# Another schedule for decoding weights and for fill matmuls in the attention stage of a fused attention and gated MLP kernel

## The chip, the core and the metric

The kernel runs on one core of a Trainium2 chip. The metric is device time in microseconds (us) of one execution; the kernel before took 1249.73 us (median of three runs, 1249.0 to 1255.0). The core's engines are called PE (matrix multiply; PEld its weight loads), DVE (vector), ACT (activation), POOL (GpSimd) and SP, whose queue issues every transfer here.

## What is computed

Random-feature attention, then a gated MLP on its output, all in float32; the MLP's weights come as float64.

```python
proj = q_or_k @ w_phi                        # 8 batches x 8 heads, 576 rows, 64 -> 128 features
proj = proj - max(abs(proj), axis=-1)
phi  = concat([exp(proj), exp(-proj)])       # 256 features
kv, z = phi(k).T @ v, sum(phi(k))            # per head
x  = (phi(q) @ kv) / (phi(q) @ z + 1e-6)     # then as 4608 tokens x 512
xn = x / sqrt(mean(x*x) + 1e-6) * rms_g
out = (silu(xn @ w_gate) * (xn @ w_val)) @ w_out      # 512 -> 1536 -> 512
```

## The kernel before, in words

There are three stages. The attention stage handles two heads of a batch at a time, a *pair*; 32 pairs (`PR`) go through a pipeline of four steps in a loop of 35 *rounds*. In round i, `front(i)` transposes q and k of pair i (L298), projects them (L311 to L313: three matmuls, since float32 is split in a high and a low part), and takes the row maximum (L315) and the difference (L318) on DVE. `mid(i-1)` makes the exponentials on ACT (L341, L345, L381, L382), the low parts of the q features on POOL (L386, L388), and phi(k).T v on PE (L349, L354), whose result is split by L60 and L61. `back(i-2)` multiplies with phi(q) (L421), copies the result out (L424, L429), and sends the denominators through memory for a reciprocal (L431, L438, L440, L441, L443). `last(i-3)` scales on DVE (L458, L459) and stores 576 tokens of x.

Two kinds of work of the second stage ride along in these rounds:

- *Decoding.* The float64 weights are turned into float32 by integer operations. A *piece* is one 128 x 384 block: a load of 384 KB (L37), two passes on ACT (L48, L49), three on DVE (L50 to L52), two on POOL (L54) and a last sum on DVE (L55). There are 32 pieces. The first eight are kept in SBUF as operands of the fills: for them `fill_w` adds a scaling by g (L234) and a split (L60 on ACT, L61 on DVE, tiles fg and fv). The other 24 are stored to memory (L240) and are read back later, for the first time by L157 and L161 (`raw_gv`, tile wc).
- *Fills.* A *unit* is twelve matmuls of 256 columns (L490), a product of 256 finished tokens with 128 decoded columns of w_gate or w_val, copied out by ACT (L493) and stored (L494). Six units belong to a block of 256 tokens, which is loaded (L507) and split (L60, L61, tile xo) once. 54 units are done in the attention stage and the other 54 after it.

How many of each go in a round is set by three statements of the loop: `dq` adds up a quota of pieces per round, `FIRST` is the first round with fills, and `quota` spreads 40 units evenly over the rounds from `FIRST` to 31 and 14 over the last three. `_merge` sorts the round's pieces of work by a position between 0 and 1 and issues them in that order. On top of that the framework's scheduler reorders instructions by its own estimates of durations; so it also puts two DVE operations on tile wc, which belong to the next stage, into the attention rounds. Every engine runs its own instructions strictly in the order that results.

The second stage (L566, L1041 to L1076) does the rest of the fills and the gated product by a Strassen-Winograd scheme with 7 products; the third (L1257) is the product with w_out.

Of the kernel before, what the change touches and what calls it, by code (L numbers as in the profile page):

```python
# [63 lines left out]
def _merge(streams):  # L64


    todo = []
    for n, st in enumerate(streams):
        for i, piece in enumerate(st):
            at = (i + 0.5) / len(st)  # L70
            if isinstance(piece, tuple):
                at, piece = piece
            todo.append((at, n, i, piece))
    for _, _, _, piece in sorted(todo, key=lambda t: t[:3]):
        piece()


def _spread(pieces, a, b):
    return [(a + (b - a) * (n + 0.5) / len(pieces), p) for n, p in enumerate(pieces)]
# [3 lines left out]
def kernel(ctx: ExitStack, tc: tile.TileContext, q, k, v, w_phi,  # L83
# [14 lines left out]
    J1 = 3  # L98
# [54 lines left out]
    def raw_gv(j):  # L153

        raws[j] = w = wst.tile([128, 5, 2, 128], F32, name="wc")
        cs = slice((J1 + j) * 128, (J1 + j + 1) * 128)
        nc.sync.dma_start(out=w[:, 0:2].rearrange("p o c f -> p (o c) f"),  # L157
                          in_=wgs[:, cs].rearrange("(c p) f -> p c f", p=128))
        vv = wvs[:, cs].rearrange("(k c p) f -> k p c f", p=128, c=2)
        for k in range(2):  # L160
            nc.sync.dma_start(out=w[:, 3 - k], in_=vv[k])  # L161
# [90 lines left out]
    def decode_pieces(jobs, dec):  # L252
        raws = {}

        def piece(i):
            if i == 0:
                raws[0] = _fetch(nc, dec, *jobs[0][:2])
            raw = raws.pop(i)
            if i + 1 < len(jobs):
                raws[i + 1] = _fetch(nc, dec, *jobs[i + 1][:2])  # L260
            with late():
                jobs[i][2](_decode(nc, dec, raw, jobs[i][1], nc.gpsimd if i >= 2 * NC + 24 else nc.vector))
        return [lambda i=i: piece(i) for i in range(len(jobs))]
# [3 lines left out]
    def load(pr):  # L267
        b, hp = divmod(pr, NP)
        h0 = 2 * hp
        kt = ld.tile([128, 2, T0, D], F32, name="kt")  # L270
        qt = ld.tile([128, 2, T0, D], F32, name="qt")
        for dst, src in ((kt, k), (qt, q)):
            nc.sync.dma_start(out=dst.rearrange("p h t d -> p h (t d)"),
                              in_=src[b, h0:h0 + 2, 0:SM, :].rearrange("h (p t) d -> p h (t d)", t=T0))
        rb = ld.tile([128, 2, D], F32, name="rb")
        vm, vr = vms[pr % 3], vrs[pr % 3]
        for i, src in enumerate((k, q)):
            nc.sync.dma_start(out=rb[:, i], in_=src[b, h0:h0 + 2, SM:S, :])
        for hh in range(2):
            nc.sync.dma_start(out=vm[:, hh, :, 0:D], in_=v[b, h0 + hh, 0:SM, :].rearrange("(p t) d -> p t d", t=T0))  # L280
            nc.sync.dma_start(out=vr[hh * 64:(hh + 1) * 64, hh, 0:D], in_=v[b, h0 + hh, SM:S, :])
        st[pr] = dict(kt=kt, qt=qt, rb=rb, hp=hp, b=b, vm=vm, vr=vr, kv=kvs[pr % 2])
# [167 lines left out]
    def last(pr):  # L450
        d = st.pop(pr)
        nd, rc, b, hp = d["nd"], d["rc"], d["b"], d["hp"]

        def fin():
            xt = nd[0]
            eng = nc.gpsimd if pr == PR - 2 else nc.vector
            with late():
                eng.tensor_tensor(xt[0:64], nd[0][0:64], rc[:, 0], ALU.mult)  # L458
                eng.tensor_tensor(xt[64:128], nd[1][0:64], rc[:, 1], ALU.mult)  # L459
            r0, c0 = hp * 128, b * S  # L460
            if b % 2 == 0:
                nc.sync.dma_start(out=xs[r0:r0 + 128, c0:c0 + S], in_=xt)
            else:
                nc.sync.dma_start(out=xs[r0:r0 + 128, c0:c0 + SR], in_=xt[:, SM:S])
                nc.sync.dma_start(out=xs[r0:r0 + 128, c0 + SR:c0 + S], in_=xt[:, 0:SM])
            if hp == NP - 1:
                while blocks and blocks[0] * TF + TF <= (b + 1) * S:
                    fills.append(blocks.pop(0))

        return [(0.65, fin)]  # L470
# [25 lines left out]

    early = decode_jobs()
    decs = decode_pieces(early, dec)
    RES, FIRST, TAIL = 9 * J1 * 2, 9, 14
    units, here = [], []  # L500
    dq = quota = 0.0

    def load_x():
        while fills and len(here) < 2:
            bk = fills.pop(0)
            x = fxp.tile([128, NC, TF], F32, name="x")
            nc.sync.dma_start(out=x, in_=xsv[:, :, bk * TF:(bk + 1) * TF])  # L507
            here.append((bk, x))
# [3 lines left out]
    def landed(lo_eng=nc.vector):  # L512
        if here:
            units.extend(fill(*here.pop(0), lo_eng, [fp, fp]))
# [4 lines left out]
    for i in range(PR + 3):  # L519
        streams = []  # L520
        if i < PR:
            streams.append(_spread(front(i), -0.2, 0.7))
        if 0 <= i - 1 < PR:
            streams.append(_spread(mid(i - 1), -0.2, 1.1))
        if 0 <= i - 2 < PR:
            streams.append(back(i - 2))
        if 0 <= i - 3 < PR:
            streams.append(last(i - 3))
        dq += 0.8 if i < 10 else 1.1
        dl, decs = decs[:int(dq)], decs[int(dq):]  # L530
        dq -= int(dq)
        streams.append(dl)
        if i < PR:
            _merge(streams)
        if len(units) <= 6:
            landed(nc.vector if i < PR else nc.gpsimd)
        if i >= FIRST:
            quota += (N // TF * J1 * 2 - RES - TAIL) / (PR - FIRST) if i < PR else TAIL / 3
            nf = min(int(quota + 1e-6), len(units))
            quota -= nf  # L540
            now, units[:] = units[:nf], units[nf:]
            _merge([now] if i < PR else streams + [_spread(now, 0.0, 0.75)])
        load_x()
        if i + 2 < PR:
            load(i + 2)
        if i in (20, 22):
            raw_gv((i - 20) // 2)
# [780 lines left out]
```

## Time and profile before

| what | value |
|---|---|
| median of the runs | 1249.73 us |
| the profiled execution's own time | 1250.33 us |
| its span, first to last instruction | 1248.6 us |
| PE busy | 1216.2 us (97%) |
| DVE, ACT, POOL busy | 1034.0, 803.3, 830.8 us |
| mean granted PE clock | 0.991 |
| end of the attention stage, about | 507 us |

The profile gives busy times of each engine, the chain of work that ended last, groups of instructions with what ended the idle time before them, and tables of stretches in which the number behind an x counts instructions. Ends of matmuls are modelled, so a busy PE may still be waiting for short times; the count of matmuls in a stretch is the better measure there.

### The profile page before, as it was taken

To read this page: it belongs to the slowest core of one execution; us is meant where nothing else is said; L and a number is where in the kernel's file an instruction comes from. 1 tells how busy PE (TensorE), PEld (TensorE's weight loads), DVE (VectorE), ACT (ScalarE), POOL (GpSimd) and SP (SyncE) were. 2 spreads that over 40 slices of the span, in tenths; PEclk is the share of its full clock that TensorE was granted. 3 is DMA by queue.
4 is the path that set the end of the run, shared out by engine and by line. 5 is a ranking of instruction groups with operands and counts; after the bars stand their busy time and mean duration, and the time that the engine had idled before them with its cause. 6 is when DMAs were issued, how large, how long until landed. Compare 5 with 4: busy or idle time off the path is not lost.

```text
span 1248.6 us, 28447 instructions
## 1 busy us (share of the span) xinstructions
PE 1216.2 (97%) x10355; PEld 1204.6 (96%) x10355; DVE 1034.0 (83%) x1498; ACT 803.3 (64%) x1867; POOL 830.8 (67%) x756
## 2 busy tenths in 40 slices
PE   8999999999999998999999999999999899999998
PEld 7988999999999998999999999999999899999998
DVE  6888987678788886588996888978775889999995
ACT  6888887768788786667666576667655443433432
POOL 3655654446556666675776766687655578888885
PEclk9999999989999998999999999999999899999999
DMA  5455565756665654686455666556544545444531
GB/s 152 129 133 157 140 204 152 182 159 170 176 172 142 177 153 148 211 249 210 137 191 187 202 199 209 167 199 201 171 153 136 178 148 162 147 135 141 166 117 51
DMA packets 214344, 206.55 MB, mean 165 GB/s; under 512 B 70334, under 2 KB 176702, under 8 KB 214204
## 3 DMA queue, kind: packets, MB, share of 16 engines
q1 hardware_dynamic: 214204, 204.73, 53.9%
q8 instruction: 82, 1.34, 0.5%
q14 instruction: 58, 0.48, 0.1%
HBM read 135.18 MB, written 69.49 MB: 164 GB/s over the span
## 4 chain that ended last, share of the span: by engine, by line
PE 83%; DVE 7%; DMA 4%; issue 2%; ACT 1%; POOL 1%; SPq 1%; DVEq 0%; ACTq 0%; POOLq 0%
PE B L566 12%; PE E L566 11%; PE A L566 11%; PE acc L354 6%; PE fp L490 5%; PE gd L1257 5%; PE gz L1257 5%; PE gy L1257 5%; PE sm L421 5%; PE fp L1257 3%; PE pp L311 2%; PE pp L313 2%; PE pp L312 2%; PE sm L370 2%; PE sm L298 2%
## 5 line engine op out<-in xcount | busy, mean ns | idle before, releaser
L386 POOL TENSOR_TENSOR ql<-eq,qh 128x256 fp32r<-128x256 f32 x256 | 216.4, 875 | 92.9 <-issue 57.6
L566 PE MATMUL B<-xo,w 128*128 128x256 f32 x1458 | 194.2, 277 | 3.5 <-DVE c L566 2.4
L566 PEld LDWEIGHTS B<-xo,w 128*128 128x128 f32 x1458 | 178.7, 188 | 5.1 <-DVE c L566 3.4
L61 POOL TENSOR_TENSOR xo<-st,xo 128x768 fp32r<-128x768 f32 x52 | 122.4, 2366 | 35.4 <-ACT xo L60 31.7
L315 DVE TENSOR_REDUCE mx<-pp 128x4 f32<-128x512 f32 (+1 forms) x160 | 101.0, 633 | 49.9 <-PE pp L313 48.3
L60 ACT CAST xo<-st 128x768 fp32r<-128x768 f32 x54 | 43.6, 837 | 150.1 <-DVE st L1207 69.7
L566 PE MATMUL A<-xo,w 128*128 128x256 f32 x972 | 137.0, 277 | 0.0
L566 PE MATMUL E<-xo,w 128*128 128x256 f32 x972 | 136.9, 277 | 0.0
L354 PE MATMUL acc<-vm,ek 128*128 128x65 f32 x1024 | 129.8, 268 | 0.0
L566 POOL TENSOR_TENSOR h<-h,c 128x256 f32<-128x256 f32 x81 | 64.7, 799 | 91.9 <-ACT h L566 73.1
L354 PEld LDWEIGHTS acc<-vm,ek 128*128 128x128 f32 x1024 | 125.8, 192 | 0.0
L566 PEld LDWEIGHTS A<-xo,w 128*128 128x128 f32 x972 | 122.6, 188 | 0.3
L566 PEld LDWEIGHTS E<-xo,w 128*128 128x128 f32 x972 | 122.5, 188 | 0.1
L382 ACT ACTIVATE qh<-sm 128x512 fp32r<-128x512 f32 (+1 forms) x192 | 96.8, 504 | 0.0
L61 POOL TENSOR_TENSOR xo<-w,xo 128x768 fp32r<-128x768 f32 x36 | 91.0, 2527 | 7.4 <-ACT xo L60 7.4
L311 PE MATMUL pp<-wh,th 128*128 128x256 f32 x288 | 87.9, 307 | 4.1 <-DVE yq L318 1.7
L381 ACT ACTIVATE eq<-sm 128x512 f32<-128x512 f32 x128 | 78.2, 611 | 18.6 <-PE sm L370 17.9
L313 PE MATMUL pp<-wh,tl 128*128 128x256 f32 x288 | 84.2, 301 | 0.2
L312 PE MATMUL pp<-wl,th 128*128 128x256 f32 x288 | 82.1, 286 | 0.0
L566 ACT ACTIVATE h<-A 128x256 f32<-128x256 f32 x81 | 31.1, 384 | 76.8 <-PE A L566 63.3
L388 POOL TENSOR_TENSOR ql<-eqr,qh 128x256 fp32r<-128x256 f32 x32 | 25.5, 797 | 81.5 <-ACT qh L382 74.3
L1257 PE MATMUL gy<-w,xo 128*128 128x256 f32 x648 | 78.3, 279 | 0.5 <-ACT xo L60 0.5
(190 smaller groups left out, 3601.9 us busy)
## 6 DMA issues: line engine op xcount, KB each, us to landing
w<-hs SPq DMA_DIRECT2D x17, 1536.0 KB
hs<-h SPq DMA_DIRECT2D x81, 256.0 KB
gvs<-fo SPq DMA_DIRECT2D x108, 128.0 KB
gvr<-gvs SPq DMA_DIRECT2D x54, 256.0 KB
x<-xs SPq DMA_DIRECT2D x18, 512.0 KB
x<-xs SPq DMA_DIRECT2D x9, 1024.0 KB
rc<-di SPq DMA_DIRECT2D x31, 288.0 KB
kt<-in_k_dram SPq DMA_DIRECT2D x32, 256.0 KB
```

The lines of the kernel that those rows point to most:

```text
L61: (lo_eng or nc.vector).tensor_tensor(lo, x, hi.bitcast(F32), ALU.subtract)
L311: nc.tensor.matmul(o, th[:, cs], wh, start=True, stop=False)
L312: nc.tensor.matmul(o, th[:, cs], wl, start=False, stop=False)
L313: nc.tensor.matmul(o, tl[:, cs], wh, start=False, stop=True)
L315: nc.vector.tensor_reduce(mx[:, 0:2 * m], pp[:, 0:2 * m], axis=AX.X, op=ALU.max, apply_absolute_value=True)
L354: nc.tensor.matmul(acc[:, sg, h], e[h][:, sg, j], vm[:, h, j], start=False, stop=(h == 1 and j == T0 - 1))
L381: nc.scalar.activation(ei[:, sg], yi, AF.Exp, scale=1.0 - 2.0 * sg)
L382: nc.scalar.activation(hi[:, sg], yi, AF.Exp, scale=1.0 - 2.0 * sg)
L386: nc.gpsimd.tensor_tensor(lo[:, sg, cs], ei[:, sg, cs], hi[:, sg, cs].bitcast(F32), ALU.subtract)
L421: nc.tensor.matmul(o[:, 0:m], a[:, h, sg], e[:, sg, h, cs], start=(i == 0), stop=(i == 5))
L566: r = f(*a, **k)
L1257: nc.tensor.matmul(place[n], a[:, kp], w[:, o], start=(first and (kp, i) == turns[0]), stop=((kp, i) == turns[-1]), skip_group_check=True)
```

## The change

The decoding quota is 0 for the first two rounds, 0.75 pieces a round for the next eleven and 1.27 after that, where it was 0.8 for ten rounds and 1.1 after that. Fills begin with round 12 in place of round 9, so that the 40 units lie on 20 rounds, two in each, where they lay on 23 rounds, one or two in each. Numbers of pieces, units and instructions stay as they are.

```diff
-    RES, FIRST, TAIL = 9 * J1 * 2, 9, 14
+    RES, FIRST, TAIL = 9 * J1 * 2, 12, 14
...
-        dq += 0.8 if i < 10 else 1.1
+        dq += 0 if i < 2 else 0.75 if i < 13 else 1.27
```

Two places show what this does to the order of instructions. On DVE, from the third pair on (a full-width L315 is one of the four in each pair's projections), this stood before:

```order
L315 TENSOR_REDUCE mx<-pp 128x4
L50 TENSOR_SCALAR wp<-wa 128x384
L318 TENSOR_TENSOR yq<-pp,mx 128x512
L51 SCALAR_TENSOR_TENSOR wp<-wa,wp 128x384
L315 TENSOR_REDUCE mx<-pp 128x2
L52 TENSOR_SCALAR wa<-wp 128x384
L318 TENSOR_TENSOR yr<-pp,mx 128x256
L61 TENSOR_TENSOR tl<-sm,th 128x512
L55 TENSOR_TENSOR wa<-wp,wa 128x384
L234 TENSOR_SCALAR wa<-wa,g 128x384
```

and this stands there now:

```order
L315 TENSOR_REDUCE mx<-pp 128x4
L318 TENSOR_TENSOR yq<-pp,mx 128x512
L315 TENSOR_REDUCE mx<-pp 128x2
L61 TENSOR_TENSOR tl<-sm,th 128x512
L318 TENSOR_TENSOR yr<-pp,mx 128x256
L61 TENSOR_TENSOR tl<-sm,th 128x512
L315 TENSOR_REDUCE mx<-pp 128x4 x2
L318 TENSOR_TENSOR yk<-pp,mx 128x512 x2
```

The first piece (L50 to L55, L234) is gone from here. Counted in full-width L315, the eight fill_w pieces began after 2, 2.5, 3.5, 4.75, 6.5, 7.5, 8.5 and 9.5 pairs; they begin now after 3.5, 4.5, 5.5, 7.5, 8.5, 9.5, 12 and 12.75 pairs. The first L490 stood in the eleventh pair and stands now in the fourteenth.

The second place is SP's queue between the store of the last decoded block that raw_gv needs (L240) and the loads of it (L161). Before:

```order
L465 DMA xs<-nd 128x512
L240 DMA wvs<-wa 128x384
L441 DMA di<-dr 128x9
L37 DMA raw<-in_moe_w_val_dram 128x768
L507 DMA x<-xs 128x4x256
L494 DMA gvs<-fo 128x256
L443 DMA rc<-di 64x1152
L280 DMA vm_145<-in_v_dram 128x4x64
L273 DMA qt<-in_q_dram 128x2x256
L431 DMA dd<-nd 1x576
L281 DMA vr_148<-in_v_dram 64x64
L161 DMA wc<-wvs 128x2x128 x2
```

and now, two rounds later:

```order
L240 DMA wvs<-wa 128x384
L464 DMA xs<-nd 128x64
L465 DMA xs<-nd 128x512
L441 DMA di<-dr 128x9
L280 DMA vm_147<-in_v_dram 128x4x64 x2
L443 DMA rc<-di 64x1152
L281 DMA vr_150<-in_v_dram 64x64
L507 DMA x<-xs 128x4x256
L494 DMA gvs<-fo 128x256
L273 DMA qt<-in_q_dram 128x2x256
L161 DMA wc<-wvs 128x2x128
L431 DMA dd<-nd 1x576
```

Here the loads kept their place in the round: in both, the second load is the tenth transfer behind L441. The raw load (L37) moved ahead of this piece, and a small transfer (L431) now stands between the two loads. On DVE the operation that waits for both loads stands after the second yk of its round, before and now:

```order
L61 TENSOR_TENSOR tl<-sm,th 128x512
L315 TENSOR_REDUCE mx<-pp 128x4
L318 TENSOR_TENSOR yk<-pp,mx 128x512
L566 TENSOR_TENSOR wc<-wc 128x256 x2
L50 TENSOR_SCALAR wp<-wa 128x384
L315 TENSOR_REDUCE mx<-pp 128x4
```

(these rows are of the change; before, the last two stood the other way round). Nothing moved around the two L566 rows but that. Behind the attention stage the engines' rows are nearly the same.

## The prediction

> **What bounds the kernel now.** The page's busy times and its chain of waits come first, to see which engine sets the end.
>
> ```profile
> PE 1216.2 (97%) x10355; PEld 1204.6 (96%) x10355; DVE 1034.0 (83%) x1498; ACT 803.3 (64%) x1867; POOL 830.8 (67%) x756
> PE 83%; DVE 7%; DMA 4%; issue 2%; ACT 1%; POOL 1%; SPq 1%; DVEq 0%; ACTq 0%; POOLq 0%
> ```
>
> PE is busy for 97% and makes 83% of the chain. The change neither adds nor removes a matmul, so it can only gain or lose what PE stands still, and only in the attention stage, which it rearranges. The table of stretches shows where that is. I cut it where the transposition of each pair's last rows begins, for the pairs that matter, and took the rest in longer pieces; the number behind PE's x counts its matmuls.
>
> ```profile
> core 0: us, PE busy (x) PEld busy (x) DVE busy (x) ACT busy (x) POOL busy (x), PEclk, DMA share, GB/s
> 22.60:34.90 12.30, 12.30 (x108) 12.30 (x106) 10.91 (x21) 11.15 (x26) 7.91 (x12) 1.00 0.69 190
> 34.90:50.80 15.90, 13.63 (x113) 13.08 (x113) 13.85 (x26) 15.10 (x40) 11.97 (x16) 1.00 0.39 95
> 50.80:62.60 11.80, 11.74 (x101) 11.54 (x101) 10.70 (x21) 9.99 (x26) 7.42 (x10) 1.00 0.54 145
> 62.60:76.00 13.40, 12.84 (x109) 12.44 (x108) 12.65 (x24) 10.48 (x28) 7.25 (x9) 1.00 0.52 133
> 76.00:90.20 14.20, 13.53 (x113) 13.10 (x113) 11.95 (x22) 11.72 (x30) 6.74 (x9) 1.00 0.44 128
> 90.20:105.70 15.50, 13.53 (x108) 12.56 (x107) 12.83 (x23) 12.81 (x33) 9.32 (x13) 1.00 0.68 188
> 105.70:119.70 14.00, 13.25 (x109) 12.72 (x107) 13.32 (x25) 11.28 (x28) 8.18 (x9) 1.00 0.57 155
> 119.70:131.00 11.30, 11.21 (x91) 10.78 (x92) 11.20 (x20) 9.87 (x26) 10.05 (x12) 1.00 0.37 100
> 131.00:146.40 15.40, 15.08 (x126) 14.62 (x125) 14.74 (x28) 13.40 (x35) 8.26 (x12) 1.00 0.63 159
> 146.40:162.20 15.80, 15.80 (x138) 15.80 (x137) 12.03 (x23) 14.07 (x36) 10.53 (x15) 1.00 0.59 160
> 162.20:179.30 17.10, 17.10 (x149) 17.10 (x148) 13.00 (x25) 13.24 (x34) 7.71 (x12) 1.00 0.67 204
> 240.00:260.00 20.00, 16.97 (x121) 16.27 (x120) 11.57 (x21) 10.84 (x29) 8.79 (x11) 0.83 0.69 178
> 260.00:480.00 220.00, 219.49 (x1870) 218.56 (x1869) 180.26 (x318) 177.30 (x446) 130.30 (x159) 1.00 0.57 160
> 480.00:507.00 27.00, 22.23 (x163) 21.33 (x162) 18.22 (x18) 13.55 (x34) 17.91 (x20) 0.87 0.64 209
> ```
>
> From 260 to 480 us PE is never idle for long and does 1870 matmuls in 220 us, 8.5 a microsecond. Taking that as its full pace, the loss of a row is its length less its count over 8.5. In order, the first eleven rows lose -0.4, 2.6, -0.1, 0.6, 0.9, 2.8, 1.2, 0.6, 0.6, -0.4 and -0.4: 8.8 us up to 146.4, 8.0 with the two rows of fills behind. The stretch from 240 to 260 loses 20 - 14.2 = 5.8, the one from 480 on 27 - 19.2 = 7.8. So there are three places: the early rounds (which the change aims at), one stall in the middle, and the end of the stage.
>
> The waits of PE between 20 and 150 us tell who makes it wait in the early rounds, in total, times and longest.
>
> ```profile
> PE sm L370 <- DVE yq L318: 1.9, 3, 1.4
> PE fp L421 <- DVE kv1l L61: 1.6, 2, 1.2
> PE pp L311 <- DVE yk L318: 0.7, 1, 0.7
> ```
>
> It is DVE, which in those rows is busy for 80 to 99% of the time.
>
> **The early pieces.** Their price on DVE comes from its groups between 20 and 150 us.
>
> ```profile
> L234 DVE TENSOR_SCALAR wa<-wa,g 128x384 f32<-128x384 f32 x8 | 6.1, 759 | 0.1
> L51 DVE SCALAR_TENSOR_TENSOR wp<-wa,wp 128x384 int32<-128x384 int32 x8 | 5.8, 726 | 0.1
> L55 DVE TENSOR_TENSOR wa<-wp,wa 128x384 f32<-128x384 f32 x8 | 5.8, 722 | 0.8 <-POOL wa L54 0.8
> L50 DVE TENSOR_SCALAR wp<-wa 128x384 int32<-128x384 int32 x8 | 4.4, 549 | 0.9 <-ACT wa L48 0.9
> L52 DVE TENSOR_SCALAR wa<-wp 128x384 int32<-128x384 int32 x8 | 3.2, 406 | 0.1
> L61 DVE TENSOR_TENSOR fg<-wa,fg 128x384 fp32r<-128x384 f32 x4 | 2.2, 561 | 0.0
> ```
>
> One fill_w piece is 759 + 726 + 722 + 549 + 406 + 561 ns, 3.7 us. DVE is busy for 10.7 us of the 11.8 us round in which no piece begins, so a round can hardly take a piece without growing: 3.7 us in each of eight are 29.8 us of DVE work, of which 8.8 us came through to PE, 1.1 a piece. Where the pieces begin shows in the same table for L50 alone (DVE time and count).
>
> ```profile
> 34.90:50.80 15.90, 1.66 (x2) 1.00 0.39 95
> 50.80:62.60 11.80, 0.00 (x0) 1.00 0.54 145
> 62.60:76.00 13.40, 0.35 (x1) 1.00 0.52 133
> ```
>
> Two pieces begun in one round cost 2.6; a single one 0.6 (62.6), 0.9, 0.6 and 0.6; the round without one nothing. The two expensive rounds after that, 2.8 and 1.2, follow each other with a piece that starts at the very end of the row before and one that reaches over.
>
> The change moves the first piece from pair 2 to 3.5, breaks up the double, and leaves two gaps (after 5.5 and after 9.5 pairs). The price of a lone piece, the mean of the four rows named, is 0.7. Eight pieces, of which the last (12.75 pairs) runs into the first fills, where rows with pieces lose nothing (146.4, 162.2): 7 x 0.7 = 4.9 us in place of 8.0, a gain of **3.1 us**. Its bounds: no loss at all, -8.0; and 1.2 us in each of ten rounds without fills, 12 - 8 = +4 (the second rival). I take the lone piece because six of the eight pieces are now a full pair apart, as those four were. ACT's and POOL's parts lie beside: they are busy for 80 to 95% and 47 to 75% of these rows, and PE names ACT as releaser only for small waits.
>
> **Fills three rounds later.** A unit is twelve matmuls and costs PE the same wherever it stands:
>
> ```profile
> 148.72 1.36 PE fp L490 x12
> ```
>
> Six units (the old schedule's count up to round 12) leave rounds 9 to 12 and spread over the next 20, +0.35 us a round there and -8.2 us here: zero in sum as long as PE is the bound in both places. It is at full pace in the late rounds; in rounds 10 and 11, which have neither fill nor piece now, the row at 50.8 (lost -0.1) is the model.
>
> **Decoding at 1.27 a round.** The later pieces carry no L234 and no split (groups of DVE, 270 to 470 us):
>
> ```profile
> L55 DVE TENSOR_TENSOR wa<-wp,wa 128x384 f32<-128x384 f32 x15 | 12.2, 816 | 0.6 <-POOL wa L54 0.6
> L51 DVE SCALAR_TENSOR_TENSOR wp<-wa,wp 128x384 int32<-128x384 int32 x15 | 8.7, 578 | 0.1
> L50 DVE TENSOR_SCALAR wp<-wa 128x384 int32<-128x384 int32 x15 | 6.3, 421 | 8.8 <-ACT wa L48 8.8
> L52 DVE TENSOR_SCALAR wa<-wp 128x384 int32<-128x384 int32 x15 | 5.8, 388 | 0.1
> ```
>
> 816 + 578 + 421 + 388 = 2.2 us. 0.17 pieces more a round are 0.37 us of DVE, where it has 220 - 180.3 = 39.7 us free over some 14 rounds, 2.8 each. Zero; if that cover were gone, 14 x 0.37 = 5 us.
>
> **The stall in the middle.** The scheduler put L566 on tile wc into the round whose transfers bring it. The rows are of the timelines of DVE, SP's queue, PE twice, and of PE's stretch 250 to 260.
>
> ```profile
> 245.10 0.76 DVE L566 TENSOR_TENSOR wc<-wc 128x256 f32<-128x256 f32 x2 [5.33 <-DMA wc<-wvs]
> 240.29 1.39 SPq L161 DMA_DIRECT2D wc<-wvs  x2
> 249.66 0.35 PE L311 MATMUL pp<-wh,th 128*128 128x256 f32 x1 [1.71 <-DVE yq L318]
> 253.18 1.12 PE L370 MATMUL sm<-ident,yq 128*128 128x128 f32 x4 [1.31 <-DVE tl L61]
> 250.00:260.00 10.00, 8.69 (x54) 0.66 0.67 182
> ```
>
> DVE waits 5.33 us for a load issued at 240.29, just after DVE was ready for it; L315 and L318 queue behind, PE stops for 1.71 and 1.31 us, and its granted clock falls to 0.66 over the ten microseconds. Of the 5.8 us lost, 3.0 are those two stops and 2.8 the clock and shorter waits. In the new order the loads wait for a block that is decoded two rounds later, and the DVE operation has moved with them to the same place in its round. So the stall stays: 0, with bounds of -5.8 (gone) and, if the load comes one issue of 0.7 us (1.39 for two) later, +0.7.
>
> [...]
>
> **The end of the stage, and after.** PE's longest wait there is
>
> ```profile
> 495.14 0.58 PE L421 MATMUL sm<-qh,kv1h 128*128 128x256 f32 x1 [4.44 <-ACT nd L424]
> ```
>
> It hangs on the reciprocal of pair 29 on its way through memory. The last rounds keep their 14 units, and the transfers of that way keep their sequence: zero, give or take 1. The two stages behind are not touched.
>
> **Sum.** The profiled execution took 1250.33 us, 1248.6 of them its span and 1.7 around it. 1250.3 - 3.1 = 1247.2; the median lies 0.6 below the profiled one, so the forecast is **1246.6 us**.
>
> **Rivals.**
>
> *The stall shrinks.* If L161 is issued a little earlier against DVE, PE never stops long enough, and 2.8 to 5.8 us more go: 1240.8 to 1243.8. For it: the raw load of 384 KB is out of the way of these loads now. Against: the load of x (512 KB) comes closer to them.
>
> *It is the missing fill that idles PE.* Rounds from 62.6 to 131 lost 6.1 us in five, 1.2 each, and the one at 105.7 lost its 1.2 though no piece begins in it; the rounds with fills lost nothing though they have as many pieces. Then not decoding but the lack of matmuls that depend on nothing is at fault: in the chain from projection over DVE to transposition PE has nothing else to do. Without fills to round 12 there are ten such rounds (3 to 12) at 1.2, 12.2 in place of 8.0: +4.2, 1253.9, slower. It decides from 8 us of loss before the first unit on. Against it stands the row at 50.8.
>
> *The early loss goes altogether*, since DVE can catch up between lone pieces: -8.0, 1241.7.
>
> *Nothing changes*, the price being 1.1 for each of eight pieces wherever they lie: 1249.7. That the order does not follow the quotas is excluded by the rows shown.
>
> **How the numbers follow.** The forecast has 0.40 (its own range 1243.5 to 1250), the shrunken stall 0.18, the missing fill 0.18, the early loss gone 0.12, nothing 0.12. About 0.5%, 6.2 us, is what a measurement of this kernel can tell from no change. Faster than 1243.5: most of the second and of the fourth case and an edge of the first, 0.32. Slower than 1256: the upper half of the missing fill, together with a somewhat longer stall, 0.10. The rest, 0.58, is the same. The range 1238 to 1255 takes in all cases, the missing fill together with a somewhat longer stall, and most of the way to the stall and the early loss both gone (1250.3 - 8.0 - 5.8 - 0.6 = 1235.9).
>
> **What would show it.** Right: between 20 us and the first L490, matmuls over 8.5 fall short of the time by some 5 us in place of 8.8; the round of the second and third L50 is not longer than the others; L566 on wc still waits about 5 us for its load, two rounds later; 260 to 480 us stays at 8.5 matmuls a microsecond. Wrong: early rounds that lose as much without a piece as with one, a wait of DVE on wc below 3 us or above 7, or a new stop of PE of over 1 us after 150 us.

## The result, and the profile after

The changed kernel takes 1258.95 us (median of 19 runs, 1253.06 to 1265.47), the kernel before 1251.88 us (19 runs beside them, 1247.11 to 1262.05). The ratio is 1.0051, interval 1.0029 to 1.0073: slower by about 6.4 us, where 3.1 us of gain were forecast. The profiled execution took 1257.4 us, its span 1255.6, which is 7.0 more than before. The ratios here and below leave out the executions that ran over 1.5% above the fastest of their kernel, six in all, of which two (2033 and 1723 us) had a mean granted clock of 0.65.

The page's busy times and the shares of its chain, after:

```profile
PE 1216.9 (97%) x10355; PEld 1205.0 (96%) x10355; DVE 1038.9 (83%) x1498; ACT 805.1 (64%) x1867; POOL 828.6 (66%) x756
PE 81%; DVE 9%; issue 3%; DMA 3%; ACT 2%; POOL 1%; SPq 0%; DVEq 0%; ACTq 0%; POOLq 0%
```

PE does the same work, and DVE's share of the chain rose from 7 to 9%. To see where the 7 us arose, I cut the attention stage of both kernels by rounds: 0 and 1, from 2 until the fills run at pace (to round 13 before, to round 14 after), to 21, to 30, and the rest. A row has PE's busy time, its count of matmuls behind the x, the granted clock, the DMA share and GB/s. Before:

```profile
0.00:22.60 22.60, 17.23 (x105) 1.00 0.55 142
22.60:194.90 172.30, 165.46 (x1371) 1.00 0.56 152
194.90:329.70 134.80, 131.77 (x1106) 0.97 0.63 172
329.70:462.40 132.70, 132.19 (x1123) 1.00 0.61 167
462.40:507.00 44.60, 39.84 (x313) 0.92 0.47 154
```

And after:

```profile
0.00:22.80 22.80, 17.69 (x105) 1.00 0.55 145
22.80:208.20 185.40, 174.72 (x1452) 1.00 0.54 141
208.20:325.00 116.80, 114.66 (x982) 1.00 0.65 182
325.00:464.50 139.50, 137.82 (x1169) 1.00 0.60 168
464.50:514.00 49.50, 40.99 (x311) 0.90 0.51 157
```

The loss of a row is its length less its count over 8.5, as in the prediction. The five rows lost 10.2, 11.0, 4.7, 0.6 and 7.8 us before, and 10.4, 14.6, 1.3, 2.0 and 12.9 after: +0.2, +3.6, -3.4, +1.4 and +5.1, together +6.9. The two later stages took 741.6 us in both. So the stall in the middle shrank, and the early rounds and the end of the stage, one expected to gain and the other to stay, both lost.

**The early rounds.** In the same table, cut by rounds, round 5 stands out (17.4 - 113/8.5 = 4.1 lost; 4.4 in the lists by round below, where a matmul that reaches over an edge is counted once), between two that lost nothing:

```profile
49.20:60.80 11.60, 11.60 (x102) 1.00 0.57 146
60.80:78.20 17.40, 13.72 (x113) 1.00 0.47 121
78.20:90.00 11.80, 11.71 (x101) 1.00 0.53 151
```

The timeline of DVE in that round, and PE's two longest waits there:

```profile
61.38 0.36 DVE L50 TENSOR_SCALAR wp<-wa 128x384 int32<-128x384 int32 x1 [0.61 <-ACT wa L48]
61.77 0.56 DVE L51 SCALAR_TENSOR_TENSOR wp<-wa,wp 128x384 int32<-128x384 int32 x1
62.85 0.91 DVE L52 TENSOR_SCALAR wa<-wp 128x384 int32<-128x384 int32 x1
64.29 1.27 DVE L318 TENSOR_TENSOR yq<-pp,mx 128x512 f32<-128x512 f32 x2
65.48 1.30 DVE L458 TENSOR_TENSOR nd<-nd,rc 64x576 f32<-64x576 f32 x1
66.80 1.19 DVE L459 TENSOR_TENSOR nd<-nd,rc 64x576 f32<-64x576 f32 x1
68.02 0.43 DVE L61 TENSOR_TENSOR kv1l<-acc,kv1h 128x260 fp32r<-128x260 f32 x1
```

```profile
64.03 0.41 PE L421 MATMUL fp<-qh,kv1h 128*128 128x320 f32 x1 [1.12 <-ACT kv1h L60]
68.50 0.42 PE L421 MATMUL fp<-qh,kv1l 128*128 128x320 f32 x1 [2.28 <-DVE kv1l L61]
```

It is a lone piece: the next one begins at 77.1. PE began with kv1h at 64.03; the 0.43 us that make kv1l from it stood on DVE behind the piece's L50 to L52 and behind L458 and L459, and PE could not go on without it. The first of the two waits is ACT's: the last matmul into acc had ended at 60.9, but kv1h, made from acc, came on ACT at 63.60, behind the piece's two passes L48 and L49 (1.0 us) and four exponentials.

**The stall** is still there, DVE waiting for the second load, but shorter (3.75 us, before 5.33), and PE stopped once in place of twice:

```profile
274.44 0.89 DVE L566 TENSOR_TENSOR wc<-wc 128x256 f32<-128x256 f32 x2 [3.75 <-DMA wc<-wvs]
PE sm L370 <- DVE tl L61: 2.1, 1, 2.1
280.00:285.00 5.00, 2.86 (x25) 1.00 0.59 182
```

The granted clock stayed at 1.00; before, it had fallen to half at 250.72 us, for 6.8 us.

**The end of the stage.** PE, which had one long stop there, now has two:

```profile
492.29 0.66 PE L370 MATMUL sm<-ident,yq 128*128 128x128 f32 x4 [2.13 <-ACT nd L429]
501.31 0.58 PE L421 MATMUL sm<-qh,kv1h 128*128 128x256 f32 x1 [4.83 <-ACT nd L424]
```

ACT's L429 waited for an nd buffer whose store came late:

```profile
ACT nd L429 <- DMA xs<-nd: 2.8, 1, 2.8
```

The store waits for L458 and L459. On DVE they stand behind the last piece's L55 now (the rows after):

```profile
484.12 0.69 DVE L318 TENSOR_TENSOR yq<-pp,mx 128x512 f32<-128x512 f32 x1
484.73 0.79 DVE L55 TENSOR_TENSOR wa<-wp,wa 128x384 f32<-128x384 f32 x1
485.44 1.28 DVE L458 TENSOR_TENSOR nd<-nd,rc 64x576 f32<-64x576 f32 x1
```

Before, they stood ahead of it, 18.6 us after the row's start against 20.9 now (L55 itself is 0.8 of these 2.3 us; the yq ahead of it is late too):

```profile
480.39 0.69 DVE L318 TENSOR_TENSOR yq<-pp,mx 128x512 f32<-128x512 f32 x1
481.00 0.98 DVE L458 TENSOR_TENSOR nd<-nd,rc 64x576 f32<-64x576 f32 x1
483.35 0.85 DVE L55 TENSOR_TENSOR wa<-wp,wa 128x384 f32<-128x384 f32 x1
```

### The profile page after: what moved, and what is told of

Its sections match the earlier page's. It is cut to its first block, busy times and chain, and to the rows that moved or that the text cites. A ratio compares the mean times of both kernels' runs of the same rounds, so it can differ in the third digit from the quotient of the medians.

```text
span 1255.6 us, 28459 instructions
## 1 busy us (share of the span) xinstructions
PE 1216.9 (97%) x10355; PEld 1205.0 (96%) x10355; DVE 1038.9 (83%) x1498; ACT 805.1 (64%) x1867; POOL 828.6 (66%) x756
## 4 chain that ended last, share of the span: by engine, by line
PE 81%; DVE 9%; issue 3%; DMA 3%; ACT 2%; POOL 1%; SPq 0%; DVEq 0%; ACTq 0%; POOLq 0%
PE B L566 13%; PE E L566 11%; PE A L566 11%; PE acc L354 6%; PE fp L490 6%; PE gy L1257 5%; PE gd L1257 5%; PE gz L1257 5%; PE sm L421 4%; PE fp L1257 2%; PE pp L311 2%; PE pp L313 2%; PE pp L312 2%; PE sm L370 2%; PE sm L298 2%
## 5 line engine op out<-in xcount | busy, mean ns | idle before, releaser
L566 PE MATMUL B<-xo,w 128*128 128x256 f32 x1458 | 194.2, 277 | 2.0 <-DVE c L566 1.9
L566 PEld LDWEIGHTS B<-xo,w 128*128 128x128 f32 x1458 | 178.8, 188 | 3.4 <-DVE c L566 2.9
L315 DVE TENSOR_REDUCE mx<-pp 128x4 f32<-128x512 f32 (+1 forms) x160 | 100.6, 632 | 46.1 <-PE pp L313 44.4
L566 PE MATMUL A<-xo,w 128*128 128x256 f32 x972 | 137.0, 276 | 0.0
L566 PE MATMUL E<-xo,w 128*128 128x256 f32 x972 | 136.8, 276 | 0.0
L566 POOL TENSOR_TENSOR h<-h,c 128x256 f32<-128x256 f32 x81 | 65.3, 806 | 90.0 <-ACT h L566 68.4
L566 PEld LDWEIGHTS A<-xo,w 128*128 128x128 f32 x972 | 122.7, 188 | 0.3
L566 PEld LDWEIGHTS E<-xo,w 128*128 128x128 f32 x972 | 122.5, 188 | 0.1
L566 ACT ACTIVATE h<-A 128x256 f32<-128x256 f32 x81 | 31.3, 386 | 75.4 <-PE A L566 60.9
L1257 PEld LDWEIGHTS gy<-w,xo 128*128 128x128 f32 x648 | 76.8, 191 | 1.6 <-ACT xo L60 1.4
```

What stands on the lines that cost most here:

```text
L315: nc.vector.tensor_reduce(mx[:, 0:2 * m], pp[:, 0:2 * m], axis=AX.X, op=ALU.max, apply_absolute_value=True)
L566: r = f(*a, **k)
L1257: nc.tensor.matmul(place[n], a[:, kp], w[:, o], start=(first and (kp, i) == turns[0]), stop=((kp, i) == turns[-1]), skip_group_check=True)
```

## The experiments

The table gives, for the profiled execution of each kernel, the loss by stretch in the way just shown (early: from round 2 to the round in which fills run at pace, 13 or 14; middle: to round 21; late: 22 to 30; end: 31 to the last fill), and the ratio of its runs to those of the kernel before on the same chip.

| kernel | early | middle | late | end | ratio (95% interval) |
|---|---|---|---|---|---|
| before | 11.0 | 4.7 | 0.6 | 7.8 | 1 |
| changed | 14.6 | 1.3 | 2.0 | 12.9 | 1.0051 (1.0029 to 1.0073) |
| changed, again | 15.4 | 1.9 | 1.1 | 12.4 | 1.0066 (1.0038 to 1.0095) |
| fills late only | 15.2 | 2.0 | 0.9 | 7.1 | 1.0006 (0.9975 to 1.0038) |
| lone pieces | 24.9 | 2.0 | 0.4 | 8.4 | 1.0007 (0.9982 to 1.0031) |
| bare early rounds | 2.3 | 9.6 | 1.5 | 5.9 | 0.9955 (0.9915 to 0.9995) |
| changed, six nd buffers | 16.5 | 4.8 | -0.2 | 3.3 | 1.0042 (1.0011 to 1.0073) |
| before, no stall | 12.1 | -1.4 | 0.4 | 7.6 | 0.9975 (0.9952 to 0.9998) |
| before, POOL | 17.8 | 5.6 | 0.3 | 8.5 | 1.0075 (1.0043 to 1.0107) |
| changed, 1.5 pieces late | 16.3 | 4.5 | 2.9 | 7.8 | 1.0048 (1.0026 to 1.0071) |
| changed, no stall | 18.7 | -1.3 | 1.0 | 11.3 | 1.0026 (0.9987 to 1.0064) |
| changed, no stall, pieces first | 10.2 | 2.3 | 1.0 | 11.5 | 1.0010 (0.9978 to 1.0041) |
| before, no stall, pieces first | 8.5 | -1.0 | 0.4 | 7.4 | 0.9956 (0.9921 to 0.9991) |
| before, no stall, pieces last | 13.6 | 0.2 | 1.5 | 6.7 | 0.9969 (0.9942 to 0.9995) |

**The changed kernel again.**

> The changed kernel unaltered, beside the kernel before on the same chip, for a second profile of it: which of its losses come again. Theory: the waits that follow from the order come again (the stop of about 2 us in the round of the second and third piece, DVE's wait of 3.5 to 5.5 us on wc, PE's two stops of about 2 and 5 us at the end of the stage), so the stage loses 40 to 46 us, the end of it 11 to 14. Rival: the losses at the end are chance of one execution: 8 to 9 us there this time. Ratio to the kernel before 1.003 to 1.007.

The early loss, DVE's wait on wc (4.4 us), PE's stops (2.7 us there, 1.8 and 4.8 at the end) and the loss at the end came again within 1 us, so they follow from the order and are no chance of one execution. Single rounds differ more: round 8 lost 3.6 us in place of 1.9, with the granted clock at half for 3.4 us.

**Half of the change: fills late, decoding as before.**

```diff
-    RES, FIRST, TAIL = 9 * J1 * 2, 9, 14
+    RES, FIRST, TAIL = 9 * J1 * 2, 12, 14
```

> The kernel before with the first fill round moved from 9 to 12 and the old decoding quota. Loss is again length less matmuls over 8.5 a microsecond. Theory A (a piece costs PE something only in a round without fills, about 1.3 to 1.6 us each, a round without a piece costs nothing): the ten pieces that now begin before the first fill lose 12 to 15 us between 22 us and the first L490, where before 11 were lost by eight; +1 to +4 us there. Theory B (each round without a fill loses 1.2 us, piece or not): eleven such rounds, 13 us, and rounds without a piece lose as much as the others. Prediction's own price of 0.7 us for each lone piece: 9 to 10 us. End of the stage and the stall on wc: if they are set by the fills they come out as in the changed kernel (13 and 2.4 us), if by the decoding as before (8 and 6 us).

```profile
22.80:190.00 167.20, 157.59 (x1292) 1.00 0.56 148
464.30:508.20 43.90, 39.13 (x313) 0.96 0.49 156
```

Up to round 9 it repeats the kernel before, round by round (2.9 us in round 3, 3.1 in round 7); then rounds 10 to 12, which had fills and lost 0.7 us together, lose 1.4, 1.7 and 1.1 without them. So the later fills alone cost 4 us in the early rounds. The end stays at 7.1: what the end lost in the changed kernel comes from the decoding quota. The other half alone cannot be had, since fills in round 9 need eight decoded pieces.

**Lone pieces**, one in each round from the third on:

```diff
-        dq += 0.8 if i < 10 else 1.1
+        dq += 0 if i < 2 else 1.0 if i < 10 else 1.1
```

> The kernel before with decoding beginning in round 2 at exactly one piece a round to round 9, 1.1 after that, fills from round 9 as before: eight lone pieces, one in each round from 2.5 to 9.75 pairs, no double. The prediction's price of a lone piece (0.7 us): 8 x 0.7 = 5.6 us lost between 22 us and the first L490, some 5 us less than the 11 before, ratio about 0.996. Theory A (1.3 to 1.6 us for each piece without fills, whether alone or not): 10 to 13 us, no gain, ratio 0.998 to 1.002. Theory B: eight or nine rounds at 1.2, 10 to 11 us.

All three expectations were too low for this execution, the slowest of its kernel: 24.9 us, of which rounds 5, 7 and 12 lost 7.5, 4.1 and 8.5. PE stopped there for kv1l or kv0l (2.3 us in round 5), and in rounds 5 and 12 the granted clock fell to half, for 6.8 and 10.2 us:

```profile
67.00:72.00 5.00, 2.71 (x20) 0.92 0.49 148
72.00:77.00 5.00, 5.00 (x24) 0.50 0.38 115
PE fp L421 <- DVE kv1l L61: 2.3, 1, 2.3
DVE nd L458 <- DMA vm<-in_v_dram: 3.5, 1, 3.5
```

The last row is of round 12. There DVE had done the piece's L50 to L52 and stood idle ahead of L458, waiting for a transfer (named vm; the load that L458 reads from is rc, issued at 167.25 behind two loads of x). So that round's 4.3 us of stop are not the price of a piece. 0.7 us for a lone piece is refuted; over the runs the kernel is no faster than the kernel before.

**Neither pieces nor fills early.**

```diff
-    RES, FIRST, TAIL = 9 * J1 * 2, 9, 14
+    RES, FIRST, TAIL = 9 * J1 * 2, 20, 14
...
-        dq += 0.8 if i < 10 else 1.1
+        dq += 0 if i < 13 else 1.5
...
-        if i in (20, 22):
-            raw_gv((i - 20) // 2)
+        if i in (28, 30):
+            raw_gv((i - 28) // 2)
```

> The kernel before with no decoding in rounds 0 to 12 (1.5 pieces a round after that), fills from round 20 on, and the first raw loads of the next stage in rounds 28 and 30: ten rounds with neither a piece nor a fill. Theory A: those rounds, 3 to 12, lose less than 0.3 us each, below 2 us in all, and take 11.6 to 12.4 us, the matmuls' own time. Theory B (it is the missing fill that idles PE): 1.2 us each, 10 to 12 us in all. The total says little, as all 32 pieces press on the later rounds: 1250 to 1280 us.

```profile
24.40:175.90 151.50, 149.69 (x1268) 1.00 0.51 133
```

Twelve rounds lose 2.3 us, 0.2 each: rival B, the missing fill, falls. Theory A's bounds were a little too narrow (rounds 3 to 12 lose 2.6 us, a single one up to 1.0). What the pieces cost comes back where they now stand: 9.6 us in the middle, nearly all in rounds 14 to 19, which have few fills yet. That the kernel is some 0.45% faster than before was not expected (its losses sum to 31.2 us where the kernel before has 34.3), and the interval is wide; why it is faster stays open.

**Six nd buffers in the changed kernel** (one line):

```diff
-        nd = [big.tile([128, S], F32, name="nd", bufs=4) for _ in range(2)]
+        nd = [big.tile([128, S], F32, name="nd", bufs=6) for _ in range(2)]
```

> The changed kernel with six buffers of nd in place of four, so that back of a pair need not wait for the store of the pair two before it. Theory: the two long stops at the end of the stage (PE for 2.1 us behind ACT's L429, 4.8 us behind L424) both wait for an nd buffer that hangs on a reciprocal on its way through memory; with two buffers more both go, and with them the low clock behind them: the end of the stage loses 3 to 6 us in place of 13, and the kernel takes 7 to 10 us less than the changed one, ratio to the kernel before 0.997 to 1.000. Rival: the stop only moves to the next thing in the chain (the single rc buffer, the reciprocals of the last pair), and less than 3 us are gained, ratio 1.003 to 1.005.

```profile
468.30:508.30 40.00, 38.36 (x312) 1.00 0.51 155
522.70 0.84 PE L566 MATMUL A<-xo,fg 128*128 128x256 f32 x5 [3.68 <-POOL xo L566]
```

Both stops went and the end lost 3.3 us, as the theory said. But the time hardly moved: PE reached the next stage earlier and stood 3.7 us there for a split by POOL, the stall in the middle had a worse execution (4.8), and the order on DVE had changed so that the bad place of the early rounds was now in round 8 (8.0 us lost, clock at half for 10.2 us). The mechanism of the end is shown, the expected gain was given back.

**Fewer DVE operations in a piece**: L234 and the low part of the split on POOL.

```diff
-                    nc.vector.tensor_scalar(w, w, g[:, c:c + 1], None, ALU.mult)
-                    _split(nc, wf1[wi][:, 0, c], wf1[wi][:, 1, c], w)
+                    nc.gpsimd.tensor_scalar(w, w, g[:, c:c + 1], None, ALU.mult)
+                    _split(nc, wf1[wi][:, 0, c], wf1[wi][:, 1, c], w, lo_eng=nc.gpsimd)
```

> The kernel before with two of the seven DVE operations of a fill_w piece (the scaling L234 and the low part of the split, 759 and 561 ns of the 3.7 us) put on POOL. Theory A (a piece costs PE by the DVE time that it takes out of a round without fills): the piece is 2.4 us on DVE, the loss between 22 us and the first L490 falls from 11 us by a third or more, to 4 to 8 us; 3 to 6 us less in all, ratio 0.995 to 0.998. Rival: the price is not DVE's but that of ACT or of the order, since PE's waits in the changed kernel name ACT's kv1h as often as DVE's: 10 to 12 us, no change; or POOL, which feeds PE with ql, becomes late itself: 12 us or more, with waits on POOL ql.

A third less DVE time in each piece, and 17.8 us lost in place of 11.0: theory A in its form of DVE's time falls. PE has no wait on POOL's ql in the early rounds, so that rival falls too. Rounds 4, 7 and 13 lost 5.3, 3.4 and 4.1. What these rounds share with the dear ones of the other kernels is an order on DVE: kv0l or kv1l stands directly behind L458 and L459 (at most L440, of 0.2 us, between), and these behind L50 to L52 of a piece. All such rounds up to here:

| kernel | round: loss (us) |
|---|---|
| before, and with late fills | 7: 3.1 |
| changed, and again | 5: 4.4 |
| changed, 1.5 pieces late (below) | 5: 5.8 |
| lone pieces | 5: 7.5, 7: 4.1, 12: 8.5 |
| POOL | 4: 5.3, 7: 3.4, 13: 4.1 |
| six nd buffers | 8: 8.0 |

Where kv0l or kv1l stands behind the three operations alone, or still later, behind L55 and L234 too, rounds lost 0 to 2.9 us (once 3.6). This is theory K of the last experiments.

Two things limit what the table says. Much of the spread is the clock: it was at half for 3.4 us in rounds 4 and 13 of POOL and in round 5 of the kernel with 1.5 pieces, for 6.8 in round 5 of the lone pieces, and for 10.2 in their round 12 and with six buffers. With half of these times taken off, all rows lie between 2.4 and 4.4 us. And the order marks the dear rounds without explaining all of their loss: PE's stops for the kv tiles, high and low parts, make 3.4 us in round 5 of the changed kernel, 0.8 with six buffers and 0.3 in POOL's round 13.

**1.5 pieces a round late in the changed kernel.**

```diff
-        dq += 0 if i < 2 else 0.75 if i < 13 else 1.27
+        dq += 0 if i < 2 else 0.75 if i < 13 else 1.5
```

> The changed kernel with 1.5 pieces a round from round 13 on in place of 1.27, so that the last piece begins some three pairs before the end of the attention stage. Theory: the end lost 5 us more because the last pieces run into the last rounds and put off L458 of pair 28 on DVE, on which an nd buffer hangs: without pieces there the end loses 7 to 9 us as before, ratio to the kernel before 0.999 to 1.002. Rival: the end is set by the fills' order, not by pieces: 12 to 14 us again, ratio 1.004 to 1.006. A cost that would show the density itself: new losses of over 1 us a round from 200 to 400 us.

```profile
471.30:516.20 44.90, 40.70 (x315) 0.92 0.51 153
490.36 1.00 DVE L458 TENSOR_TENSOR nd<-nd,rc 64x576 f32<-64x576 f32 x1
```

Without a piece in the last rounds L458 begins 19.1 us after the row's start and the end loses 7.8 us, as before the change: the theory of the end holds. In the time nothing of it is seen; the density cost 0.9 more in the late rounds, and in the middle DVE waited 6.1 us on wc and the clock fell to half (4.5 us lost).

**No stall**: the next stage's DVE operations are held behind the attention stage's.

```diff
             self.eng, self.kind, self.last = eng, kind, None
+            if kind == mybir.EngineType.DVE:
+                self.last = next(i for i in reversed(tc.nc.cur_bb.bb.instructions) if i.engine == kind)
```

> The kernel before with the next stage's DVE operations held behind the last DVE instruction of the attention stage, so that the two L566 on wc no longer stand in the attention rounds. Theory: the stall of rounds 16 to 18 (5.8 us lost, 1.7 and 1.3 us of stops and then the low clock) is that wait and nothing else: it goes, and the stretch 240 to 260 does 170 matmuls; 4 to 6 us less than before, ratio 0.995 to 0.997, unless the next stage now waits for its first weights (then its start gives back 1 us, the two operations being 1.2 us). Rival: DVE waits for the same busy transfers elsewhere, and the gain is below 2 us.

```profile
240.00:260.00 20.00, 20.00 (x175) 1.00 0.74 206
```

175 matmuls in place of 121: the stall was that wait and nothing else. The kernel is faster than before; the ratio's middle shows 3 us of the 4 to 6 expected, which its interval holds.

> The changed kernel with the next stage's DVE operations held behind the attention stage's, as was done to the kernel before (ratio 0.9975 there). Theory: the change gained 3 to 4 us in the middle only because its stall on wc was shorter; with the stall gone in both it shows its other costs alone (early rounds +4, end +5, single rounds +1.5), so it stands 9 to 11 us behind the kernel before with the same edit: ratio to the kernel before 1.003 to 1.006, no loss from 200 to 300 us. Rival: the stall was no part of the difference, and the two with the edit differ by 6 us or less: 1.000 to 1.002.

The stall is gone here too. The two kernels with this edit stand 0.5% apart, 6.4 us, between what the theory and the rival gave, with intervals too wide to decide. This execution repeats the stops of round 5, but here the clock fell (see the last section).

**Pieces at another place of their round**, in the rounds before the first fills, together with the edit above (0.02, first, or 0.7, last; in the changed kernel i < 13):

```diff
-        streams.append(dl)
+        streams.append([(0.02, f) for f in dl] if i < 10 else dl)
```

> The changed kernel, stall removed, and the pieces of rounds 0 to 12 issued at the start of their round instead of its middle, so that on DVE kv0l and kv1l (L61) no longer stand behind L50 to L52 of a piece: before the first fill no kv row but one stands behind them, where in the changed kernel eight do. Theory K (the price of a piece is what it holds up on DVE, above all kv1l, which L421 waits for): the loss from round 2 to round 14 falls from 15 us to 7 to 10 us, PE's waits on kv1l and kv1h from 5.7 us to below 2; ratio 0.998 to 1.001. Rival D (DVE has too little time in these rounds, so the loss is the same wherever a piece stands in its round): 13 to 16 us, other waits in place of those; ratio 1.003 to 1.006.

```profile
23.80:204.70 180.90, 173.01 (x1451) 1.00 0.54 145
PE pp L311 <- DVE yr L318: 2.5, 2, 1.5
PE fp L421 <- ACT kv1h L60: 0.7, 2, 0.5
PE fp L421 <- DVE kv1l L61: 0.4, 1, 0.4
```

> The kernel before, stall removed, and the pieces of rounds 0 to 9 issued at the start of their round. Theory K: the loss from round 2 to round 13, 11.3 us in the kernel before, falls to 6 to 9; with the stall gone the ratio is 0.993 to 0.996. Rival D: 10 to 12 us, ratio 0.997 to 0.999. Two pieces now stand together in the third pair, which may cost 3 us there under both.

```profile
23.60:193.40 169.80, 163.74 (x1371) 1.00 0.56 151
```

> The kernel before, stall removed, and the pieces of rounds 0 to 9 issued late in their round, so that each begins at a full pair: kv1l stands behind L50 alone or behind L458 and L459 in three rounds, and the piece's other operations between the row maxima of the next projections. Theory K: the rounds whose kv1l stands behind L458 and L459 and a part of a piece (the fourth and the seventh pair) lose 3 us each, the others 1: 9 to 12 us in all, ratio 0.996 to 0.999. Rival D: 10 to 12 us, spread evenly.

The same pieces in the same rounds lose 10.2 instead of 14.6 us in the changed kernel, and 8.5 instead of 12.1 in the kernel before without the stall; none of these four executions had a low clock in the early rounds. (The changed kernel without the stall lost 18.7, with 10.2 us of half clock in round 5.) So about a third of the price is place: 8.5 lies in what theory K gave, 10.2 just above it, both outside of D; what makes the rest is not separated. The waits on kv1l and kv1h fell from 5.7 us to 1.1; part of them turned into waits on yr (2.5, from 1.2). Late in the round it costs 13.6, more than either theory gave: there the piece holds up the next projections (PE's waits on yk are 2.8 us, 0.7 without the move), so kv1l is not the only thing that is dear to hold up. Three rounds of the two placements again have a kv tile behind L458 and L459 (in two of them with L50 between), but not these behind L50 to L52, and lost 2.5 to 2.9: L458 and L459 count by themselves. And a strict queue has more such places: in the changed kernel with the pieces first, L440 held DVE for 3.3 us in round 20, waiting for its load (dr), and that round lost 3.3.

In the times the place does not show: 0.9956 and 0.9969 for the two placements and 0.9975 without a move have overlapping intervals, as have 1.0010 and 1.0026 in the changed kernel. The kernel before with the stall gone and the early pieces first is faster than both kernels, with 0.9956 (0.9921 to 0.9991).

## Why the prediction was wrong

**What bounds the kernel** was read rightly: PE, and only its losses in the attention stage. Matmul work and the later stages did not change.

**The early pieces** (forecast: 7 x 0.7 = 4.9 us in place of 8.0) is the step that failed first. Rounds 2 to 9 lost 11.0 us, 1.0 more than before. The lone price was the mean of four rows that lost 0.6 to 0.9, and the dear rows were explained away. The double at 34.9, which lost 2.6, is a lone piece: it runs from 36.2 to 44.9, and of the next one little but L50 lies in that row (timeline of DVE before):

```profile
49.82 0.91 DVE L50 TENSOR_SCALAR wp<-wa 128x384 int32<-128x384 int32 x1 [0.27 <-ACT wa L48]
```

Its L52, L55, L234 and split run in the row at 50.8, which the prediction took for a round without a piece and which lost nothing. A table that counts L50 tells where pieces begin, not where they lie. The row at 90.2, which lost 2.8 with a lone piece, had been put down to two pieces that follow each other. It was the one round of the kernel before in which kv1l stood behind a piece and L458 and L459; the order of DVE would have shown that, and that the change makes another such round. Lone pieces cost 0 to 4.4 us in the changed kernel, depending on what stands behind them. The row with the second and third L50, which was to be no longer than the others, is the longest (17.4 us).

**Fills three rounds later** (forecast: zero) cost 4 us in the run with late fills alone; in the changed kernel, where the pieces moved too, the rounds from 10 on lost 2.6 us more (3.3 in place of 0.7). "It is at full pace in the late rounds" was right for PE's work, but rounds with pieces lost their cover: the run with late fills alone shows 1.4, 1.7 and 1.1 us in rounds 10 to 12. In the changed kernel round 11 has neither a fill nor a new piece and loses 0.1, as the prediction said; round 10 has a piece after all, as have rounds 12 to 14, where the fills are only beginning.

**The rival of the missing fill** gave 1253.9, +4.2 in the early rounds, near the measured +3.6, but that is luck: the bare rounds refute its mechanism, since a round with neither piece nor fill loses 0.2. A fill does not feed PE; it covers a piece.

**Decoding at 1.27** (forecast: zero, 5 us if the cover were gone) lost 1.4 us in the late rounds (0.5 in the second execution), and it decided **the end of the stage** (forecast: zero, give or take 1), which lost 5.1 more, the largest miss of a single term. The step looked at the sequence of the transfers, which was all but kept, and not at what stands ahead of L458 on DVE. The run with late fills alone (7.1) and the one with the last pieces gone (7.8) show this.

**The stall** (forecast: stays, 0) shrank by 3.4 us. The wait was 3.7 us, inside the 3 to 7 that were said, but PE stopped once for 2.1 us and its granted clock stayed at 1.00: the 2.8 us that the prediction had put down to the clock and shorter waits were missing though DVE still waited. The rival of the shrunken stall came true with 2.8 to 5.8, and was outweighed. In part it is luck: with six buffers and with 1.5 pieces the changed kernel's DVE waited 5.0 and 6.1 us, the clock fell, and the middle lost 4.8 and 4.5. How long is "long enough" for a stop to lower the clock was the author's estimate, and no run shows one such length: the stop of 2.1 us left it at 1.00, while in the kernel before it fell to half at 250.72 us, behind the first stop, of 1.71 us, and ahead of the second.

**The sum** by what was measured is +3.6 - 3.4 + 1.4 + 5.1 + 0.2 = +6.9 for the forecast -3.1. The range ended at 1255 because the end of the stage had a bound of 1 us, and the 5 us named for the decoding entered neither a rival nor the range. Besides, three runs had put the median of the kernel before 2 us below that of 19.

## What to carry to other kernels

In a strict queue the price of an inserted piece of work is not its duration alone but also what stands behind it: before costing a moved instruction by a mean, look in the order for the short operation behind it that another engine waits for (here kv1l, of 0.43 us, for which PE stopped 2.28 us). A table of where a piece begins does not tell in which rows its other operations lie. Where work is moved away from cover, price the rows that lose their cover, and at the end of a stage follow each buffer back to the instruction that frees it. Where several stretches move by a few us each, count the loss of each stretch, since the total can come out near a forecast for the wrong reason.

## What was not expected of the hardware

The same stop can cost twice. In round 5 PE waited for 1.1, 0.3 and 2.3 us in the changed kernel and in its version without the stall alike, but in the one execution the granted clock stayed at 1.00, and in the other it fell to half for 10.2 us, and the round lost 8.6 instead of 4.4 us. The clock records show what differed. The kernel before has half clock from 250.72, 493.07, 981.18 and 1247.42 us on, the changed one from 497.26, 988.78 and 1255.02 on. In each of these two traces the times lie whole multiples of 3.413 us apart (71, 143 and 78; 144 and 78), and every stretch but the last, which the program's end cuts, lasts two or three times as long, 6.83 or 10.24 us. I cut each trace into windows of 3.413 us, with an edge where its clock fell. In the changed kernel such an edge cut the long stop, so that PE was idle for 44% and 39% of two windows:

```profile
63.77:67.18 3.41, 1.91 (x12) 1.00 0.53 115
67.18:70.59 3.41, 2.09 (x17) 1.00 0.54 189
```

In the version without the stall, whose clock fell at 68.31, more of it fell into one window, 52%, and the clock fell at its end:

```profile
64.90:68.31 3.41, 1.65 (x12) 1.00 0.52 126
68.31:78.55 10.24, 9.45 (x41) 0.50 0.30 101
```

Of the 695 windows at full clock between 20 and 1230 us in the traces of the kernel before and the changed one, the three in which PE was idle for 56% or more (66, 77 and 84%) were each followed by half clock, none of the 685 with less than 38%, and two of the seven between (50 and 40%). So in these two traces the least that was followed by half clock were 1.4 us of stops in one window, and the most that was not were 1.9 us.

There is also a second, slower pace of PE that the granted clock does not show. Between 640 and 780 us, in the second stage, whose order is nearly the same in both, the changed kernel and the one with late fills alone had these rows:

```profile
640.00:780.00 140.00, 139.94 (x1220) 1.00 0.63 203
```

```profile
640.00:780.00 140.00, 140.00 (x1185) 1.00 0.60 192
```

35 matmuls fewer at the same clock and without a pause: one every 118.1 ns in place of 114.8, and 281 ns for each matmul of L566 where the kernel before has 277. Such stretches stood elsewhere too: the kernel with bare early rounds did 849 matmuls from 1100 to 1200 us at clock 1.00, where the kernel before did 883, and in the changed kernel L566 took 281 ns from 514 to 540 us, where the kernel before took 276 from 515 to 540. The 35 matmuls of the rows above are 4 us, a part of the 15 us by which runs of one kernel differ. What causes the slower pace stays open.
